# Transposed x in blocks of two tokens of one head, with the states doubled on the diagonal

## The chip, the core and the metric

The kernel runs on one core of a Trainium2 chip. TensorE (PE) multiplies matrices and transposes through an identity matrix; PEld is its weight load. VectorE (DVE) and ScalarE (ACT) do elementwise work and read results from PSUM, the matmuls' result memory. GpSimd (POOL) does elementwise work in SBUF and issues the DMA transfers that cast from float32 to bfloat16. SyncE (SP) issues the transposing transfers and nearly all stores of the output. Each engine works through its own queue in order and waits for the others by semaphores.

The metric is the device time of one execution in microseconds.

## The reference: what is computed

For batch b and head h (8 of each) x is 512 tokens by 64 and the state 32 rows by 64. Tokens read the state, state rows read the tokens; the two reads are joined, and a two-layer network with GELU follows.

```python
B, H, S, Ns, D = (8, 8, 512, 32, 64)
scores  = scale * x @ state^T ;  a  = softmax(scores)  ; xread = a  @ state
scores2 = scale * state @ x^T ;  a2 = softmax(scores2) ; sread = a2 @ x
rows = concat([xread, sread], tokens)          # 544 rows a batch, 8 heads x 64 = 512 columns
out  = gelu(rows @ w_in) @ w_out               # 512 -> 2048 -> 512
```

The exponential of the scores serves both reads. The token read is folded into the network: per batch P = state @ w_in (per head), and the hidden layer is the transposed attention times P.

## The kernel before

**Layout.** A batch of x is loaded by a casting transfer (`load_x`, POOL's queue) as `xb`: partition p holds tokens 4p to 4p+3 of all heads, so for each head 4 tokens times 64 columns lie in a row (`j` is the token within the four). Heads are numbered `4 t + c` with t in 0..1 and c in 0..3.

**Scores.** A score matmul wants the contraction over the 64 columns on the partitions; to use 128 partitions two heads are put together, t = 0 and t = 1 of the same c. `sbd` holds for each batch and c a block diagonal of 128 x 64: the transposed state of head c in rows 0 to 63 and columns 0 to 31, that of head 4 + c in rows 64 to 127 and columns 32 to 63. For the transposed x the pair has to lie side by side: `rearr` (L221) lets POOL copy `xb` into `x4` (two tiles in turn), two copies for a batch, and `xtr_dma` (L276) transposes `x4` in one transfer from SP's queue into `xT`. Batch 0 has a path of its own, batch 1 is transposed on TensorE by `xtr` (L264), in 32 transposes of 64 rows. Batches 2 to 7 go through `rearr` and `xtr_dma`. `scores` (L325) then does 16 matmuls of 64 columns for a batch into two PSUM tiles `pt`, and ACT takes the exponentials into `e`.

**States.** `load_st` loads states as `st_bf`; `state_prep` (L156) transposes a batch's states on TensorE in one transpose, and DVE copies the two halves out of PSUM (L166) into the two diagonal blocks of `sbd`. `p_mm` (L435) uses the blocks of `sbd` as weights against `w_in` for P. `sbd` is set to zero at the start by one POOL memset (L95).

**The rest of a batch.** DVE normalises the attention (`norm`), a second transposing transfer turns it (`atr_dma`), `M` computes two matmuls of the hidden layer for one of 16 slices and ACT's GELU, and `X` are the seven products of a Strassen form of the second layer, with the sums of the hidden layer on DVE (`g_sum`, L637), and a quarter in a second level (`sub_a`, `sub_b`, L727). `reads_mm` (L962) are the state reads, whose right operand `xo` is `xb` with columns of ones, copied by POOL (`rearr_ones`, L235). The state rows pass through the network at the end, with weight sums of `w_in` (`sr_w`), which before lie in `x4` for the names 1 and 6.

**Order.** It is written by hand: every engine gets its instructions in the program's order. Batches 0 and 1 run interleaved in a long prologue; from batch 2 on, a loop over eight stages (p = 0..7) for each batch b does two hidden slices per stage for b, products for b - 1, and scores, normalisation and P for b + 1. In the prologue `state_prep(2, 3)` stands between `U(13)` (output matmuls of batch 0, copied out by DVE at L519) and `M(20, 21)`; `state_prep(3, B)` prepares all the remaining batches behind `M(30, 31)`. Stage 4 of batch 2 has `M(40, 41)` alone; stage 5 has `M(42, 43)`, a product, the state reads (one PSUM tile `sr`, copied by ACT at L970), the P matmuls of batch 3 (copied at L1002 by ACT and DVE) and `sub_a`. Four PSUM tiles of `ps_f` go round in the order of allocation and hold the scores, the hidden slices, the transposed states, the state reads and part of P.

POOL's queue after its transfer issues is: the pair copies of batches 2 and 3, the ones copies of batch 3, a copy that waits for the transposed x of batch 2 (`hold`, L1181), the load of the states of batches 3 to 7 (L121), and then in each batch the next load of x, the pair copies and the ones copies, spaced by `hold` copies (L1016) that wait for a GELU.

Of the kernel before, what the change touches and what calls it, by code (L numbers as in the profile page):

```python
# [10 lines left out]
BF16 = mybir.dt.bfloat16  # L11
# [6 lines left out]
def kernel(  # L18
# [8 lines left out]
    nc = tc.nc  # L27
# [6 lines left out]
    HC = H // 2  # L34
# [34 lines left out]
    sbd = persist.tile([128, B, HC, 2 * NS], BF16, name="sbd")  # L69
# [6 lines left out]
    xT0 = persist.tile([128, 4, SJ, 128], BF16, name="xT0", tag="mix2")  # L76
    sb0 = persist.tile([128, 2, 2, 2, NS], BF16, name="sb0")
# [4 lines left out]
    x4s = [persist.tile([128, SJ, HC, 128], BF16, name=f"x4_{i}") for i in range(2)]  # L82
# [12 lines left out]
    nc.gpsimd.memset(sbd, 0.0)  # L95
# [38 lines left out]
    def load_rest():  # L134
        load_w_out(4, 6)
        load_w_out(6, 8)
        load_w_in(1024, 1536)
        load_w_out(8, 12)
        load_w_in(1536, 2048)
        load_st(2, 3)  # L140
        load_x(2)
        load_w_out(12, 16)
        load_x(3)

# [11 lines left out]
    def state_prep(b0, b1, pool=ps_f, tag="f"):  # L156
        n = b1 - b0
        ps = pool.tile([128, n, HC, NS], BF16, name="st_ps", tag=tag)
        for b in range(b0, b1):
            nc.tensor.transpose(  # L160
                ps[:, b - b0, :, :].rearrange("p c n -> p (c n)"),
                st_bf[:, b, :, :].rearrange("q t d -> q (t d)"),
                ident,
            )
        for t in range(2):
            nc.vector.tensor_copy(  # L166
                out=sbd[64 * t:64 * t + 64, b0:b1, :, 32 * t:32 * t + 32].rearrange(
                    "d b c n -> d (b c) n"
                ),
                in_=ps[64 * t:64 * t + 64, :, :, :].rearrange("d b c n -> d (b c) n"),  # L170
            )
# [23 lines left out]
    def state0_p(ps):  # L195
        for t in range(2):
            h = slice(64 * t, 64 * t + 64)
            nc.scalar.copy(out=sbd[h, 0, :, 32 * t:32 * t + 32], in_=ps[h, 2, :, :])
# [7 lines left out]
    def begin(b):  # L206
        A = Att()
        atts[b] = A
        A.x4 = x4s[b % 2]
        A.xo = xos[b % 2]  # L210
        if b > 0:
            A.xT = att.tile([128, SJ, HC, 128], BF16, name="xT", tag="xT")

# [6 lines left out]

    def rearr(b, ts=(0, 1)):  # L221
        A = atts[b]
        src = xbs[b].rearrange("p (t c) (j d) -> p t c j d", t=2, d=D)
        for t in ts:
            nc.gpsimd.tensor_copy(  # L225
                out=A.x4[:, :, :, 64 * t:64 * t + 64].rearrange("p j c d -> p c j d"),
                in_=src[:, t],
            )
# [35 lines left out]
    def xtr(b, cs):  # L264
        A = atts[b]
        xv = xbs[b].rearrange("p (t c) (j d) -> p j c t d", t=2, d=D)
        ps = ps_f.tile([128, len(cs), SJ, 128], BF16, name="xT_ps", tag="f")
        for i, c in enumerate(cs):
            for j in range(SJ):
                for t in range(2):  # L270
                    nc.tensor.transpose(ps[64 * t:64 * t + 64, i, j, :], xv[:, j, c, t, :], ident)
        nc.vector.tensor_copy(
            out=A.xT[:, :, cs[0]:cs[0] + len(cs), :].rearrange("p j c n -> p c j n"), in_=ps
        )

    def xtr_dma(b):  # L276
        A = atts[b]
        nc.sync.dma_start_transpose(
            out=A.xT.rearrange("p j c n -> p (j c) n"),
            in_=A.x4.rearrange("p j c n -> p (j c n)"),  # L280
        )
# [43 lines left out]
    def scores(b, half):  # L325
# [4 lines left out]
        for ci in range(2):  # L330
            c = 2 * half + ci
            for j in range(SJ):
                nc.tensor.matmul(  # L333
                    pt[:, j, :, ci, :],
                    lhsT=A.xT[:, j, c, :],
                    rhs=sbd[:, b, c, :],
                    start=True,
                    stop=True,
                )
# [95 lines left out]
    def p_mm(b, f, tiles):  # L435
# [3 lines left out]
        for c in range(HC):  # L439
            for t in range(2):  # L440
                nc.tensor.matmul(  # L441
                    ps[t][32 * c:32 * c + 32, :],
                    lhsT=sbd[64 * t:64 * t + 64, b, c, 32 * t:32 * t + 32],
# [36 lines left out]
    def pmat00(h):  # L480
# [3 lines left out]
        for c in range(HC):  # L484
            for t in range(2):
                nc.tensor.matmul(
                    ps[t][32 * c:32 * c + 32, :],
                    lhsT=sbd[64 * t:64 * t + 64, 0, c, 32 * t:32 * t + 32],
# [325 lines left out]
    def sr_w(name):  # L814
        if name in "52":
            homes = [opool.tile([128, 2, 512], BF16, name="srw", tag="osb") for _ in range(2)]
        elif name == "7":
            t = att.tile([128, 2, 2, 512], BF16, name="srw7", tag="xT")
            homes = [t[:, 0], t[:, 1]]
        else:  # L820
            t = x4s["16".index(name)].rearrange("p j c n -> p (j c n)")
            t = t.rearrange("p (g k f) -> p g k f", g=2, k=2)
            homes = [t[:, 0], t[:, 1]]
# [310 lines left out]
    state_prep(1, 2)  # L1134
# [6 lines left out]
    xtr(1, (0, 1))  # L1141
    xtr(1, (2, 3))
# [33 lines left out]
    rearr(2)  # L1176
    xtr_dma(2)
    begin(3)
    rearr(3)
# [7 lines left out]
    state_prep(2, 3, ps_o, "o3")  # L1187
# [26 lines left out]
    M(28, 29)  # L1214
    hold_for(1, 12)
    rearr_ones(2)
    M(30, 31)
    state_prep(3, B)
# [3 lines left out]
    for b in range(2, B):  # L1222
        nb = b + 1
        for p in range(8):
# [23 lines left out]
            if b == 2 and p == 1:  # L1248
                w_diff("7")
            if p < 5 and nb < B:  # L1250
# [24 lines left out]
            if p == 0 and nb + 1 < B:  # L1275
                begin(nb + 1)
                rearr(nb + 1)
# [42 lines left out]
    g_sum(b, "3", x4s[0].rearrange("p j (u c) n -> p (j u) (c n)", u=2))  # L1320
# [36 lines left out]
```

## Time and profile before

| | us |
|---|---|
| median of three runs | 202.26 (201.78 to 202.26) |
| profiled execution | 202.25 |
| its span in the profile | 200.3 |
| TensorE busy | 193.9 (97%) |
| VectorE busy | 155.1 (77%) |
| ScalarE busy | 145.6 (73%) |
| GpSimd busy | 48.1 (24%) |
| granted TensorE clock, mean | 1.00 |

Times in the trace are microseconds from the start of the span. Matmuls are pipelined, so an engine that shows as busy may still stand for part of the time; the chain of waits and the distance between matmuls say more. In a timeline row the columns are start, duration, engine, line and operation, output and inputs with their shapes, the number of instructions merged into the row, and in brackets how long the engine stood before it and what ended that. In a row of groups there are busy time and mean duration after the bar.

### The profile page before, as it was taken

Reading aid. Unit: us, or ns where it says so; the run is one execution under the profiler, and the core shown is the slowest. Engines: PE = TensorE matmul, PEld = TensorE weight load, DVE = VectorE, ACT = ScalarE, POOL = GpSimd, SP = SyncE. Lnnn points to the kernel's source line nnn. Section 1 sums busy time; section 2 is a strip of 40 time slices with the busy share of each in tenths; the row PEclk is TensorE's granted clock in tenths of the full one; section 3 lists DMA queues with packets and bytes.
Section 4 is the critical chain, followed back from the end, with each engine's and each line's share of the span. In section 5 each row is a group of like instructions: output and inputs, shape, how many; then the busy total and the mean of one; then the engine's idle time right before and its main releaser. Section 6 shows DMA issues by size and latency. Waiting matters only on the chain.

```text
span 200.3 us, 5055 instructions
## 1 busy us (share of the span) xinstructions
PE 193.9 (97%) x2102; PEld 134.3 (67%) x2107; DVE 155.1 (77%) x279; ACT 145.6 (73%) x264; POOL 48.1 (24%) x65
## 2 busy tenths in 40 slices
PE   7899999999999999999999999999999999999993
PEld 2533544465767777767777787677776888878893
DVE  2963796969989769975997798849966897984863
ACT  3785577699896799569966997599948778775120
POOL 8972504543403444040504300030000000000000
PEclk9999999999999999999999999999999999999999
DMA  5999999976494959680797025420024010030044
GB/s 192 197 174 202 206 199 201 183 136 142 84 149 77 241 65 164 141 214 0 77 188 209 5 67 95 138 75 27 28 107 106 0 55 0 7 153 0 18 146 157
DMA packets 40567, 23.16 MB, mean 116 GB/s; under 512 B 21856, under 2 KB 39136, under 8 KB 40544
## 3 DMA queue, kind: packets, MB, share of 16 engines
q0 software_dynamic: 13984, 8.10, 29.9%
q1 hardware_dynamic: 25728, 14.22, 27.5%
q10 hardware_dynamic: 832, 0.52, 0.8%
q8 instruction: 16, 0.26, 0.5%
q14 instruction: 7, 0.06, 0.1%
HBM read 17.30 MB, written 8.91 MB: 131 GB/s over the span
## 4 chain that ended last, share of the span: by engine, by line
PE 86%; DMA 5%; POOL 4%; ACT 2%; issue 0%; DVE 0%; POOLq 0%
PE xp L647 36%; PE hp L506 26%; DMA xb<-in_x_dram 5%; PE xp L727 5%; PE op L548 3%; PE sp L866 3%; PE rp L932 3%; POOL w_in_bf L105 2%; PE op L532 2%; PE xp L773 2%; PE pt L333 2%; ACT P L1002 1%; PE p_ps L441 1%; PE sr L962 1%; POOL sbd L95 1%; POOL w_out_bf L113 1%
## 5 line engine op out<-in xcount | busy, mean ns | idle before, releaser
L513 ACT ACTIVATE g<-hp 128x512 bf16<-128x512 f32 x124 | 67.1, 614 | 17.0 <-PE hp L506 16.8
L506 PE MATMUL hp<-AT,P 128*128 128x512 bf16 x248 | 62.2, 379 | 0.0
L647 PEld LDWEIGHTS <-gsum 128*128 128x128 bf16 x416 | 40.4, 98 | 8.9 <-issue 0.4
L647 PE MATMUL xp<-ws,gsum 128*128 128x256 bf16 x320 | 38.2, 273 | 0.0
L506 PEld LDWEIGHTS <-P 128*128 128x128 bf16 x248 | 23.0, 98 | 19.4 <-ACT P L452 0.7
L647 PEld LDWEIGHTS <-g 128*128 128x128 bf16 x240 | 23.3, 98 | 4.8
L637 DVE TENSOR_TENSOR gsum<-g 128x2048 bf16<-128x2048 bf16 x14 | 17.0, 1218 | 0.6 <-ACT g L513 0.6
L225 POOL COPY x<-xb 128x1024 bf16<-128x1024 bf16 x12 | 12.2, 1044 | 18.5 <-DMA xb<-in_x_dram 18.5
L235 POOL COPY xo<-xb 128x1024 bf16<-128x1024 bf16 x12 | 12.2, 1043 | 14.1 <-PE sr L962 13.9
L647 PE MATMUL xp<-w_out_bf,g 128*128 128x256 bf16 x128 | 15.3, 273 | 0.0
L647 PE MATMUL xp<-ws,g 128*128 128x256 bf16 x112 | 13.4, 273 | 0.0
L1016 POOL COPY hold<-g 128x1 bf16<-128x1 bf16 x7 | 2.3, 334 | 42.9 <-ACT g L513 42.9
L666 DVE TENSOR_TENSOR c<-qb 128x256 f32<-128x256 f32 x6 | 2.6, 425 | 12.7 <-ACT qb L749 12.7
L548 PE MATMUL op<-w_out_bf,g 128*128 128x512 bf16 x44 | 11.0, 380 | 0.5 <-issue 0.3
L647 PE MATMUL xp<-w_out_bf,gsum 128*128 128x256 bf16 x96 | 11.5, 273 | 0.0
L666 DVE TENSOR_TENSOR oh<-xp,c 128x512 f32<-128x512 f32 x14 | 9.6, 686 | 2.4 <-PE xp L647 2.0
L1002 DVE CAST P<-p_ps 128x512 bf16<-128x512 f32 x15 | 9.4, 683 | 2.4 <-PE p_ps L441 2.4
L356 DVE TENSOR_TENSOR a<-e,ics 128x512 bf16<-128x512 bf16 x14 | 10.5, 750 | 0.5
L353 DVE TENSOR_REDUCE cs<-e 128x16 f32<-128x512 bf16 x14 | 9.5, 678 | 0.9 <-ACT e L340 0.9
L513 ACT ACT_TABLE_LOAD x7 | 9.0, 1283 | 0.1
L441 PE MATMUL p_ps<-w_in_bf,sbd 64*32 64x512 bf16 x248 | 9.0, 380 | 0.0
L637 DVE TENSOR_TENSOR gsum<-gsum,g 128x2048 bf16<-128x2048 bf16 x7 | 8.6, 1225 | 0.2
(155 smaller groups left out, 308.9 us busy)
## 6 DMA issues: line engine op xcount, KB each, us to landing
out_dram<-oh SPq DMA_DIRECT2D x15, 256.0 KB, 3.3
xb<-in_x_dram POOLq DMA_DIRECT2D x7, 512.0 KB, 7.1
out_dram<-oh SPq DMA_DIRECT2D x6, 512.0 KB, 3.1
w_in_bf<-in_moe_w_in_dram POOLq DMA_DIRECT2D x6, 256.0 KB, 11.7
out_dram<-osb SPq DMA_DIRECT2D x5, 256.0 KB, 3.0
w_out_bf<-in_moe_w_out_dram POOLq DMA_DIRECT2D x4, 256.0 KB, 7.8
w_out_bf<-in_moe_w_out_dram POOLq DMA_DIRECT2D x2, 512.0 KB, 13.3
x0f<-in_x_dram SPq DMA_DIRECT2D x3, 256.0 KB, 3.8
```

Of the source, the lines that this page charges most:

```text
L225: nc.gpsimd.tensor_copy(out=A.x4[:, :, :, 64 * t:64 * t + 64].rearrange("p j c d -> p c j d"), in_=src[:, t],)
L235: eng.tensor_copy(out=A.xo[:, :, :, 2 + 64 * t:66 + 64 * t].rearrange("p j c d -> p c j d"), in_=src[:, t],)
L356: nc.vector.tensor_tensor(out=A.a[:, :, hs].rearrange("p g (c n) -> p g c n", n=NS), in0=e4, in1=ics[:, :, :].to_broadcast((128, G, 2, NS) ...
L441: nc.tensor.matmul(ps[t][32 * c:32 * c + 32, :], lhsT=sbd[64 * t:64 * t + 64, b, c, 32 * t:32 * t + 32], rhs=w_in_bf[64 * t:64 * t + 64, c ...
L506: nc.tensor.matmul(hp, lhsT=Ps[b][:, t, m * 128:(m + 1) * 128], rhs=atts[b].AT[:, :, t, :], start=(t == 0), stop=(t == 1),)
L513: nc.scalar.activation(out=gs[b][:, m, :], in_=hp, func=AF.Gelu)
L548: nc.tensor.matmul(ops[b, j], lhsT=gs[b][:, m, j * 128:(j + 1) * 128], rhs=w_out_bf[:, m, :], start=(m == 0), stop=(m == MC - 1),)
L637: nc.vector.tensor_tensor(out=got[name], in0=x, in1=y, op=op)
L647: nc.tensor.matmul(ps[:, j - js[0], :], lhsT=lhs[:, m, 128 * j:128 * j + 128], rhs=rhs[:, m, :], start=(first and j == js[0] and m == 0), ...
L666: nc.vector.tensor_tensor(out=out, in0=x, in1=y, op=ALU.add)
L727: nc.tensor.matmul(xs[b, 0][:, at, :], lhsT=lhs[:, m, :], rhs=rhs[:, m, :], start=(start and m == 0), stop=(m == MH // 2 - 1), skip_group_ ...
L1002: copy(out=Ps[b][:, t, f * 512:(f + 1) * 512], in_=ps[t])
```

## The change

The transposing transfer reads `xb` itself. A block of 128 columns of `xb` holds two tokens of one head (64 columns each), so its transpose has token 2q of the head in rows 0 to 63 and token 2q + 1 in rows 64 to 127. For both halves to meet the state of that head, the state lies twice on the diagonal: `sbd` now has a block diagonal for each of the eight heads instead of four pairs, twice the size. The number and shape of the score matmuls stay; a score matmul now yields two tokens of one head. `rearr` and `x4` are gone.

To get a state into both halves, `state_twice` copies `st_bf` into `st2` with every state doubled: on DVE for batch 1 and for batch 2, right ahead of their transposes in the program, and on POOL for batches 3 to 7. `state_prep` then does two transposes for a batch instead of one. The preparation of batches 3 to 7 is split: batch 3 where all five were, batches 4 to 7 in stage 4 of batch 2, behind `M(40, 41)`, and there the second half is copied by ACT. The second half of `sbd` is set to zero by POOL behind `load_x(3)`. The batch-1 transposes on TensorE are 16 of 128 rows. The weight sums that lay in `x4` go to `st_bf` and an attention buffer (name 6) and to a new tile `late4` (name 1), which the last sum of the hidden layer uses too.

```diff
-    sbd = persist.tile([128, B, HC, 2 * NS], BF16, name="sbd")
+    sbd = persist.tile([128, B, H, 2 * NS], BF16, name="sbd")
+    st2 = persist.tile([128, B - 3, 2, 2, D], BF16, name="st2")
-    x4s = [persist.tile([128, SJ, HC, 128], BF16, name=f"x4_{i}") for i in range(2)]
+    late4 = persist.tile([128, 4, 512], BF16, name="late4")
-    nc.gpsimd.memset(sbd, 0.0)
+    nc.gpsimd.memset(sbd[:, 0:B // 2], 0.0)
...
         load_x(3)
+        nc.gpsimd.memset(sbd[:, B // 2:B], 0.0)
...
+    def state_twice(b0, b1, eng):
+        eng.tensor_copy(
+            out=st2[:, 0:b1 - b0].rearrange("q b t u d -> q (b t) u d"),
+            in_=st_bf[:, b0:b1].rearrange("q b t d -> q (b t) d")[:, :, None, :].broadcast_to(
+                [128, 2 * (b1 - b0), 2, D]
+            ),
+        )
-    def state_prep(b0, b1, pool=ps_f, tag="f"):
+    def state_prep(b0, b1, base, pool=ps_f, tag="f"):
         n = b1 - b0
-        ps = pool.tile([128, n, HC, NS], BF16, name="st_ps", tag=tag)
+        ps = pool.tile([128, n, H, NS], BF16, name="st_ps", tag=tag)
...
+        for b in range(n):
+            for t in range(2):
+                nc.tensor.transpose(
+                    ps[:, b, HC * t:HC * t + HC, :].rearrange("p c n -> p (c n)"),
+                    st2[:, b0 - base + b, t].rearrange("q u d -> q (u d)"),
+                    ident,
+                )
+        for u in range(2):
+            copy = nc.scalar.copy if n > 1 and u else nc.vector.tensor_copy
+            copy(
+                out=sbd[64 * u:64 * u + 64, b0:b1, :, 32 * u:32 * u + 32].rearrange(
+                    "d b h n -> d (b h) n"
                 ),
+                in_=ps[64 * u:64 * u + 64, :, :, :].rearrange("d b h n -> d (b h) n"),
             )
...
-    def rearr(b, ts=(0, 1)):
...
-    def xtr(b, cs):
+    def xtr(b, hs):
...
+        for i, h in enumerate(hs):
+            for q in range(SJ // 2):
+                nc.tensor.transpose(ps[:, i, q, :], xbs[b][:, h, 128 * q:128 * q + 128], ident)
+        nc.vector.tensor_copy(out=A.xT[:, hs[0]:hs[0] + len(hs)], in_=ps)
     def xtr_dma(b):
         nc.sync.dma_start_transpose(
-            out=A.xT.rearrange("p j c n -> p (j c) n"),
-            in_=A.x4.rearrange("p j c n -> p (j c n)"),
+            out=A.xT.rearrange("p h q n -> p (h q) n"),
+            in_=xbs[b].rearrange("p h d -> p (h d)"),
         )
...
-            c = 2 * half + ci
-            for j in range(SJ):
+            for t in range(2):
+                h = HC * t + 2 * half + ci
+                for q in range(SJ // 2):
                 nc.tensor.matmul(
-                    pt[:, j, :, ci, :],
-                    lhsT=A.xT[:, j, c, :],
-                    rhs=sbd[:, b, c, :],
+                        pt[:, 2 * q:2 * q + 2, t, ci, :],
+                        lhsT=A.xT[:, h, q, :],
+                        rhs=sbd[:, b, h, :],
...
+        elif name == "6":
+            homes = [
+                st_bf.rearrange("q (k b) t d -> q k (b t d)", k=2),
+                att.tile([128, 2, 512], BF16, name="srw6", tag="a"),
+            ]
...
-            t = x4s["16".index(name)].rearrange("p j c n -> p (j c n)")
+            homes = [late4[:, 0:2], late4[:, 2:4]]
...
-    state_prep(1, 2)
+    state_twice(1, 2, nc.vector)
+    state_prep(1, 2, 1)
...
-    rearr(2)
     xtr_dma(2)
     begin(3)
-    rearr(3)
     rearr_ones(3)
...
     U(13)
-    state_prep(2, 3, ps_o, "o3")
+    state_twice(2, 3, nc.vector)
+    state_prep(2, 3, 2, ps_o, "o3")
     M(20, 21)
...
     M(28, 29)
+    state_twice(3, B, nc.gpsimd)
     hold_for(1, 12)
     rearr_ones(2)
     M(30, 31)
-    state_prep(3, B)
+    state_prep(3, 4, 3)
...
+            if b == 2 and p == 4:
+                state_prep(4, B, 3)
...
-                rearr(nb + 1)
```

## The prediction

> **What bounds the kernel now.** I read the page's busy shares, then the chain that ended last, then single engines in time around the places that the change touches.
>
> Page, parts 1 and 4:
>
> ```profile
> PE 193.9 (97%) x2102; PEld 134.3 (67%) x2107; DVE 155.1 (77%) x279; ACT 145.6 (73%) x264; POOL 48.1 (24%) x65
> ...
> PE 86%; DMA 5%; POOL 4%; ACT 2%; issue 0%; DVE 0%; POOLq 0%
> ```
>
> TensorE is 86% of the chain; the 4% POOL and 5% DMA are one stretch at the start (memset, weight issues, the load of x[1], which lands at 19.4 us). Behind that the chain is TensorE to the end. So POOL's work is beside the path, and what counts is any moment when TensorE's in-order queue stands.
>
> The first such moment is batch 2's state preparation. TensorE, then DVE (start, us, engine, line):
>
> ```profile
> 37.60 1.04 PE L532 MATMUL op<-w_out_bf,g 128*128 128x512 bf16 x4
> 38.47 0.22 PE L160 MATMUL st_ps<-ident,st_bf 128*128 128x128 bf16 x1
> 38.53 1.89 PE L506 MATMUL hp<-AT,P 128*128 128x512 bf16 x8
> ```
>
> ```profile
> 34.62 1.23 DVE L576 TENSOR_TENSOR ws<-w_out_bf 128x2048 bf16<-128x2048 bf16 x1 [0.24 <-DMA w_out_bf<-in_moe_w_out_dram]
> 35.88 1.22 DVE L576 TENSOR_TENSOR ws<-w_out_bf,ws 128x2048 bf16<-128x2048 bf16 x1
> 37.15 0.69 DVE L519 COPY osb<-op 128x512 f32<-128x512 f32 x1
> 37.76 1.28 DVE L453 CAST P<-p_ps 128x512 bf16<-128x512 f32 x2
> 38.95 0.68 DVE L519 COPY osb<-op 128x512 f32<-128x512 f32 x1
> 39.55 0.45 DVE L166 COPY sbd<-st_ps 64x128 bf16<-64x128 bf16 x2
> ```
>
> TensorE goes from output matmuls through the state's transpose to the next without a pause, because the transpose reads loaded data. DVE is without a pause from 34.62 to 40.0 and runs about 1 us behind TensorE; its row of work begins when the last part of w_out lands (0.24 us of waiting).
>
> The second is stage 5 of batch 2 (DVE, then ACT):
>
> ```profile
> 60.10 1.29 DVE L453 CAST P<-p_ps 128x512 bf16<-128x512 f32 x2 [0.71 <-PE p_ps L441]
> 61.30 1.83 DVE L637 TENSOR_TENSOR gsum<-g,gsum 128x2048 bf16<-128x2048 bf16 x1
> 63.05 0.68 DVE L666 TENSOR_TENSOR oh<-xp,s 128x512 f32<-128x512 f32 x1
> 63.65 0.68 DVE L666 TENSOR_TENSOR oh<-xp,c 128x512 f32<-128x512 f32 x1
> ...
> 65.71 0.68 DVE L666 TENSOR_TENSOR oh<-xp,u 128x512 f32<-128x512 f32 x1
> ```
>
> ```profile
> 62.54 2.06 ACT L513 ACTIVATE g<-hp 128x512 bf16<-128x512 f32 x4 [1.28 <-PE hp L506]
> 66.40 0.38 ACT L970 COPY sraw<-sr 128x260 f32<-128x260 f32 x1 [1.80 <-PE sr L962]
> 66.75 1.56 ACT L1002 CAST P<-p_ps 128x512 bf16<-128x512 f32 x3
> ```
>
> DVE has a backlog there until 66.4; ACT is ahead and waits for TensorE (1.28 and 1.80 us). TensorE's matmuls run without a gap across this stretch.
>
> **The change part by part.**
>
> *Copies of x go.* Twelve POOL copies:
>
> ```profile
> L225 POOL COPY x<-xb 128x1024 bf16<-128x1024 bf16 x12 | 12.2, 1044 | 18.5 <-DMA xb<-in_x_dram 18.5
> ```
>
> 12 x 1.04 us leave POOL, which is 24% busy and off the path: 0. Cover isn't needed. The transposing transfers on SP can start 2.0 us earlier (x[2]: 34.19 to about 32.2); their readers are placed by TensorE's order (scores of batch 2 at 41.77, with no wait), so no gain. Nothing stands behind the transfer on SP before 37.87. DVE gains a little: its two-input operations were stretched when a POOL copy ran (1826 against 1218 ns at 61.30, 1509 against 692 at 78.04, 1962 against 682 near batch 4's weight sums): 0.61 + 0.82 + 1.28 = 2.7 us of DVE, which is 0% of the chain: 0. The Trainium skill ("SBUF — State Buffer", Who interferes with whom) says that a DVE instruction with two SBUF inputs is locked out while a GpSimd instruction reads SBUF; these rows agree with it, and by that rule alone, were DVE the pace, the kernel would gain 2.7 us.
>
> *TensorE work.* State transposes go from 7 to 14; five took 0.44 us and one 0.22, so 55 ns for each further one. By place: +1 at 14.8, +1 at 38.5, -3 at 48.3 (two instead of five), +8 at 62.8: +0.39 us. x[1]: 32 half-width transposes took 1.08 us, 28 ns each; 16 full ones at the 56 ns of the attention transposes (8 in 0.61 us) take 1.06: 0. Scores and P keep number and shape.
>
> *Batch 1's states (14.8 us).* The new doubling copy on DVE falls into its 1.77 us of idleness. The two copies out of PSUM are 64x256: 64x128 takes 220 ns and 64x640 takes 483, so 286, +0.13 in all before the next weight load. TensorE then waited 0.23 us for x[1] to land, which hides it: +0.05 (0 to 0.2).
>
> *Batch 2's states (38.5 us).* The doubling copy is a DVE instruction, and in the built program it stands behind both output copies and the P casts; TensorE's transposes wait for it, and all matmuls behind them in its queue too. DVE comes to it at 39.55. Price of 128x256: the nearest rows are a 128x512 bf16 copy at 350 ns and a 64x128 one at 220; I take 0.25. From DVE's end to TensorE's start 0.05 to 0.22 us (other handovers: 6.03 to 6.08, 15.85 to 16.07). So 39.55 + 0.25 + 0.2 = 40.0 instead of 38.47, and one transpose more: +1.6 (1.4 to 1.75). ACT (which waits for these matmuls, 0.57 us) and DVE move along, so nothing is won back. The clock shows 1.00 here. "TensorE: Matmul & The Clock Gate" (What's actually happening) lets the clock fall after an idle window of about 3.4 us; 1.6 us is short of it; were it to fall, some 3.4 us at half speed would add 1.7.
>
> *The earlier transfer.* The DMA engines are saturated until 36 us. In the trace's packet records the transposed x[2] moves from 35.7 to 39, and while x[3] ran beside it, x[3]'s packets fell from 366 to 278 in a microsecond. Two microseconds earlier it meets the last 1.0 us of w_out, whose landing starts DVE's row of work above. Ends: 0, and 2.2 us (the whole transfer's time when alone, 37 to 39). I take 0.4, near the tail's own length: of that 1 us, less than half is lost to sharing. DVE, and through it the wait above, shift by this.
>
> *States 3 to 7.* The POOL doubling copy (1280 elements at 1.04 us per 1024: 1.3) follows their load, issued at 41.40, landed by 46; with the pair copies gone it can be issued at about 39.5. TensorE asks at 48.1: hidden, by 2 us even if x[3] lands 1 us later. Three transposes fewer here: -0.17. The second half of the memset (1.80 us on POOL) lies in its 7.31 us of waiting before 32.15: 0.
>
> *States 4 to 7, now in stage 4 of batch 2.* Eight transposes between matmul pairs (+0.44), into one of the four rotating PSUM buffers; then a DVE copy of one half and an ACT copy of the other, and ACT's waits for DVE's (the built program's semaphore says so). ACT's next two GELUs, then the read-out copy and the P copies stand behind it. In times of before: DVE's sum takes 1.22 with POOL's copy gone, so DVE reaches the copy at 65.1; 64x1024 at 0.51 ns per element, 0.68: 65.8. ACT's half: 128x256 takes 372 ns and 128x512 some 590, so 1.0: 66.9. Two GELUs (0.51 each): 67.95; the read-out copy: 68.3; the first P copy: 68.85. The P matmuls need these buffers in this order, and the quarter products, at 67.39 before, need the first P copy: 69.0. +1.6, the 0.44 included (0.44 if DVE's copy comes at once; 2.2 if the sum stays at 1.83).
>
> *New homes for weight sums* (state buffer, an attention buffer, a new tile): the attention buffer's last reader is a transfer issued at 127.58, landing within 4.8; the sum is at 138.8: 0.
>
> Sum: 0.05 + 1.6 + 0.4 - 0.17 + 1.6 = +3.5. The profiled execution took 202.25 us (span 200.3), the median is 202.26, so 205.7.
>
> **The rivals.**
> - *One of the two waits is covered*: 204.2 without batch 2's wait (0.05 + 0.06 + 0.4 - 0.17 + 1.6 = 1.9), 204.6 if ACT's late GELUs cost only the transposes (2.3). For it: ACT had 3.1 us of idle time in that stage. Against: the buffers rotate in order, so TensorE meets that delay at the next P.
> - *Nothing waits*: only TensorE's count stays, +0.39: 202.6, within the bound. It needs DVE to reach the doubling copy by 38.2, 1.3 us earlier than its row of work allows.
> - *Faster*: DVE, relieved of POOL's copies, sets the pace somewhere that the chain doesn't show; 2.7 us of stretched operations less 0.39: 199.9. It decides if the stretched operations gate TensorE; against it, TensorE has no gap behind any of them.
> - *The transfer delays w_out's tail by up to its whole 2.2 us*: 205.7 + 1.8 = 207.5. For it: saturated engines; against: only the tail is left by then.
>
> **How the numbers follow.** Forecast 0.62; one wait covered 0.15; long collision 0.13; nothing waits 0.05; faster 0.05. A difference under 0.3% (0.6 us) can't be told from no change. Slower: 0.62 + 0.15 + 0.13 = 0.90; same 0.05; faster 0.05. All low ends together give +1.7 (203.9), all high ends +6.2 (208.4); with the covered wait below and the long collision above I take 203.6 to 207.8.
>
> **What would show it.** TensorE idle of 1.4 us or more before the transposes of batch 2's states, ended by DVE; ACT idle some 2 us in stage 4 of batch 2, ended by DVE's copy into sbd, then P matmuls waiting for ACT; x[2]'s transposing transfer issued near 32 us; DVE's three stretched operations back at 1218, 692 and 682 ns; from stage 6 of batch 2 on, the same spacing as before, shifted. The forecast is wrong if TensorE shows no wait at either place, or if its stages 3 to 7 get shorter.

## The result, and the profile after

The changed kernel takes 205.39 us (204.91 to 205.83) beside 202.06 us for the kernel before on the same chip: 1.0165 times as long, with a 95% interval of 1.0136 to 1.0195. It is slower, by 3.3 us. The forecast was 205.7. The profiled execution took 205.57 us with a span of 203.6, against 202.25 and 200.3.

Page of the changed kernel, parts 1 and 4:

```profile
PE 195.5 (96%) x2093; PEld 135.0 (66%) x2098; DVE 153.8 (76%) x282; ACT 146.6 (72%) x265; POOL 39.3 (19%) x55
...
PE 83%; DVE 8%; ACT 4%; DMA 2%; issue 1%
```

POOL lost 8.8 us of work and DVE 1.3, which moved nothing. TensorE is busy for 1.6 us longer, but its share of the chain fell from 86% to 83%, and DVE, 0% before, now has 8% and ACT 4% instead of 2%: other engines hold TensorE up. The timelines show where. TensorE of the changed kernel, at three places (start, us, engine, line and operation, the bracket is the time for which it stood):

```profile
37.20 1.04 PE L531 MATMUL op<-w_out_bf,g 128*128 128x512 bf16 x4
39.42 0.28 PE L171 MATMUL st_ps<-ident,st 128*128 128x128 bf16 x2 [1.19 <-DVE st L159]
...
49.33 0.28 PE L171 MATMUL st_ps<-ident,st 128*128 128x128 bf16 x2
50.44 1.91 PE L646 MATMUL xp<-ws,g 128*128 128x256 bf16 x16 [0.84 <-DVE P L1215]
...
63.84 1.03 PE L505 MATMUL hp<-AT,P 128*128 128x512 bf16 x4
64.70 0.61 PE L171 MATMUL st_ps<-ident,st 128*128 128x128 bf16 x8
...
69.42 1.33 PE L440 MATMUL p_ps<-w_in_bf,sbd 64*32 64x512 bf16 x24 [0.21 <-ACT g L512]
70.68 0.62 PE L726 MATMUL xp<-w_out_bf,g 128*128 128x128 bf16 x8
```

The same places in the kernel before, as far as the prediction did not show them:

```profile
48.31 0.44 PE L160 MATMUL st_ps<-ident,st_bf 128*128 128x128 bf16 x5
48.59 0.60 PE L647 MATMUL xp<-ws,g 128*128 128x256 bf16 x4
...
61.91 1.89 PE L506 MATMUL hp<-AT,P 128*128 128x512 bf16 x8
67.39 0.61 PE L727 MATMUL xp<-w_out_bf,g 128*128 128x128 bf16 x8
```

From starts like these the whole difference can be added up. Each distance is a start less an earlier start.

| stretch of TensorE's queue | before | after | difference |
|---|---|---|---|
| start to the output matmuls `U(13)` | 37.60 | 37.20 | -0.40 |
| `U(13)` to the transposes of batch 2's states | 0.87 | 2.22 | +1.35 |
| to the transposes of batch 3's states | 9.84 | 9.91 | +0.07 |
| to the products `X(1, "4")` of batch 1 | 0.28 | 1.11 | +0.83 |
| to `M(40)`, stage 4 of batch 2 | 13.32 | 13.40 | +0.08 |
| `M(40)` to the quarter products `sub_a`, stage 5 | 5.48 | 6.84 | +1.36 |
| to the end of the span | 132.9 | 132.9 | 0 |

The sum is +3.29, which is the difference of the spans. Three stretches carry it. The first and the third are waits that the prediction has; the middle one, 0.83 us, it does not have.

DVE of the changed kernel at these places:

```profile
33.67 1.36 DVE L575 TENSOR_TENSOR ws<-w_out_bf 128x2048 bf16<-128x2048 bf16 x1
...
38.55 0.68 DVE L518 COPY osb<-op 128x512 f32<-128x512 f32 x1
39.15 0.22 DVE L159 COPY st<-st_bf 128x256 bf16<-128x256 bf16 x1
39.74 0.59 DVE L178 COPY sbd<-st_ps 64x256 bf16<-64x256 bf16 x2 [0.38 <-PE st_ps L171]
...
45.28 1.77 DVE L355 TENSOR_TENSOR a<-e,ics 128x512 bf16<-128x512 bf16 x1
...
63.24 1.22 DVE L636 TENSOR_TENSOR gsum<-g,gsum 128x2048 bf16<-128x2048 bf16 x1
...
67.03 0.68 DVE L178 COPY sbd<-st_ps 64x1024 bf16<-64x1024 bf16 x1
```

The doubling copy (39.15) runs only 0.22 us, but stands at the end of DVE's row of work, and TensorE starts 0.05 us behind it. The multiplication at 45.28 takes 1.77 us; the same line takes 0.69 where nothing disturbs it. What disturbs it is POOL's doubling copy of batches 3 to 7, as two experiments below show by taking it out. On POOL's timeline:

```profile
45.25 1.25 POOL L159 COPY st<-st_bf 128x1280 bf16<-128x1280 bf16 x1 [5.26 <-DVE ics L354]
```

It started 0.03 us earlier. The P casts behind that multiplication in DVE's queue come 1.1 us late, and the products of batch 1 wait for them (0.84 in the bracket above). ACT in stages 4 and 5 of batch 2:

```profile
64.47 1.08 ACT L512 ACTIVATE g<-hp 128x512 bf16<-128x512 f32 x2 [1.28 <-PE hp L505]
67.74 1.01 ACT L178 COPY sbd<-st_ps 64x1024 bf16<-64x1024 bf16 x1 [2.18 <-DVE sbd L178]
68.77 1.08 ACT L512 ACTIVATE g<-hp 128x512 bf16<-128x512 f32 x2
69.74 0.38 ACT L972 COPY sraw<-sr 128x260 f32<-128x260 f32 x1
70.00 1.60 ACT L1004 CAST P<-p_ps 128x512 bf16<-128x512 f32 x3
```

ACT stands 2.18 us for DVE's copy, and two GELUs, the copy of the state reads and the P copies follow in a row without a pause, the quarter products behind them.

### The profile page after: what moved, and what is told of

It is laid out like the page before. It is cut to its first block, busy times and chain, and to the rows that moved or that the text cites. A ratio compares the mean times of both kernels' runs of the same rounds, so it can differ in the third digit from the quotient of the medians.

```text
span 203.6 us, 5041 instructions
## 1 busy us (share of the span) xinstructions
PE 195.5 (96%) x2093; PEld 135.0 (66%) x2098; DVE 153.8 (76%) x282; ACT 146.6 (72%) x265; POOL 39.3 (19%) x55
## 4 chain that ended last, share of the span: by engine, by line
PE 83%; DVE 8%; ACT 4%; DMA 2%; issue 1%
PE xp L646 33%; PE hp L505 24%; PE op L547 5%; PE xp L726 5%; PE sp L868 3%; PE rp L934 3%; PE xp L772 2%; DMA st_f<-in_state_dram 2%; PE pt L332 1%; PE p_ps L440 1%; DVE P L452 1%; DVE a L355 1%; ACT g L512 1%; ACT P L1004 1%; PE xT_ps L259 1%
## 5 line engine op out<-in xcount | busy, mean ns | idle before, releaser
L440 PE MATMUL p_ps<-w_in_bf,sbd 64*32 64x512 bf16 x248 | 9.9, 380 | 0.3 <-ACT g L512 0.2
L451 ACT CAST P<-p_ps 128x512 bf16<-128x512 f32 x9 | 4.9, 590 | 4.8 <-PE p_ps L440 4.8
```

The source lines that it names most:

```text
L440: nc.tensor.matmul(ps[t][32 * c:32 * c + 32, :], lhsT=sbd[64 * t:64 * t + 64, b, HC * t + c, 32 * t:32 * t + 32], rhs=w_in_bf[64 * t:64 * ...
```

## The experiments

Three theories stood at first. A: TensorE's in-order queue sets the pace, and the change put separate waits into it, each of which can be taken out by itself. B: DVE's row of work is the pace, and the waits overlap, so that taking one out lets another show. C: the new layout itself is dearer, by its scores, transposes or transfers. Later two more were about the transfer (D and N, below). Times beside a run are of the same chip as the kernel before that the ratio refers to.

**The doubling copy of batch 2 early.** It is put ahead of the row of work, where DVE has time; nothing else changes.

```diff
     M(12, 13)
+    state_twice(2, 3, nc.vector)
     srt(1)
...
     U(13)
-    state_twice(2, 3, nc.vector)
     state_prep(2, 3, 2, ps_o, "o3")
```

> Only edit against the changed kernel: the DVE copy that doubles batch 2's states stands ahead of the transpose of batch 1's state read, where DVE stood idle for 1.6 us, instead of behind the two output copies. Theory A (TensorE's queue sets the pace, and the change put three separate waits into it: 1.35 us for this copy, 0.83 us for P casts that a POOL copy made late, 1.36 us in stage 4 and 5 of batch 2): the wait ahead of the state transposes near 39.4 us goes, the other two stay, time 1.35 us below the changed kernel's 205.4, so 204.0. Theory B (DVE's row of work is the pace and the waits overlap): TensorE starts these transposes earlier and waits as much longer further on; 205.0 to 205.4. Theory C (the new layout itself is dearer): 205.4.

Measured: 203.62 us (203.29 to 204.1), ratio 1.0067 (1.0041 to 1.0093). TensorE:

```profile
37.16 1.04 PE L531 MATMUL op<-w_out_bf,g 128*128 128x512 bf16 x4
38.03 0.28 PE L171 MATMUL st_ps<-ident,st 128*128 128x128 bf16 x2
```

The distance is 0.87 us as before the change, with no bracket. The stretch of stages 4 and 5 stays 6.84, so nothing came back there: this is A, and B falls. The span of this profile is 201.5, 2.1 less than with the change alone: 1.35 is this wait, and 0.77 more lies in the distance to the products of batch 1, 0.34 instead of 1.11, of which the edit says nothing; the last table of this section comes back to it.

**Both halves of the states of batches 4 to 7 copied by DVE.** ACT's copy goes; the eight transposes stay in stage 4.

```diff
-            copy = nc.scalar.copy if n > 1 and u else nc.vector.tensor_copy
+            copy = nc.vector.tensor_copy
```

> Only edit against the changed kernel: in stage 4 of batch 2 DVE copies both halves of the states of batches 4 to 7 out of PSUM, ACT none. Theory A: ACT's two GELUs no longer stand behind DVE's copy, the PSUM buffer comes free about 0.65 us after DVE's first copy, about when the P matmuls ask for it, and the quarter products start about 0.9 us earlier than in the changed kernel; the eight transposes (0.44 us) stay. 204.5. If it is the transposed states' hold on one of four rotating PSUM buffers and not ACT's wait: under 0.3 us, 205.2. Theory B: 205.0 to 205.4. Theory C: 205.4.

Measured: 204.76 us (204.16 to 204.94), ratio 1.0108 (1.0049 to 1.0167). TensorE, then ACT:

```profile
63.95 1.03 PE L505 MATMUL hp<-AT,P 128*128 128x512 bf16 x4
...
69.79 0.61 PE L726 MATMUL xp<-w_out_bf,g 128*128 128x128 bf16 x8
```

```profile
65.89 1.08 ACT L512 ACTIVATE g<-hp 128x512 bf16<-128x512 f32 x2 [0.23 <-PE hp L505]
```

The stretch falls from 6.84 to 5.84. ACT reaches its second pair of GELUs without standing for DVE. What is left over the 5.48 of before is 0.36, less than the 0.44 us of the eight transposes. The rival that the transposed states are dear by their hold on one of the four PSUM tiles (expected: under 0.3) falls with it: the tile comes free 4.57 us behind `M(40)` instead of 4.91, only 0.34 earlier. In this profile DVE stood 1.15 us for w_out and its doubling copy took 0.32, so that the first wait was 0.88 longer (3.10 us from `U(13)` to the transposes), and the distance to the products of batch 1 was 0.81 shorter; these nearly cancel, and the span of 202.7 is 0.9 below that of the changed kernel, about the 1.00 of the stretch.

**States of batches 3 to 7 loaded twice.** Two casting loads put them straight into `st2`, which grows by a batch, and POOL's doubling copy goes.

```diff
-    load_st(3, B)
+    load_st_twice(3, B, 1)
...
-    state_twice(3, B, nc.gpsimd)
...
-    state_prep(3, 4, 3)
+    state_prep(3, 4, 2)
```

```diff
+    def load_st_twice(b0, b1, at):
+        for u in range(2):
+            nc.gpsimd.dma_start(
+                out=st2[:, at:at + b1 - b0, :, u, :].rearrange("q b t d -> q (b t) d"),
+                in_=st_rows[:, b0:b1, :, :].rearrange("q b t d -> q (b t) d"),
+            )
```

> Only edit against the changed kernel: the states of batches 3 to 7 are loaded twice, straight into the doubled tile, so POOL's copy of 1280 elements is gone; one load more (about 1 us of POOL's issue time). Theory A, that POOL's copy at 45.25 us shut out a DVE operation with two SBUF inputs (1.77 us instead of 0.69) and so made P casts late: that operation is back at 0.69 us, TensorE's wait of 0.84 us near 50.4 us goes, 204.5. If the casts are late for another reason: the operation is short, the wait stays, 205.4. If the second load lands later than 49 us, the transposes of batch 3's states wait for it instead.

Measured: 204.96 us (204.53 to 205.66), ratio 1.0129 (1.0076 to 1.0181). The distance to the products of batch 1 is 0.11 us, 0.17 below the kernel before: the three transposes fewer that the prediction counted. The multiplication is back at its usual time:

```profile
46.40 0.69 DVE L362 TENSOR_TENSOR a<-e,ics 128x512 bf16<-128x512 bf16 x1
```

The time fell by only 0.4, which the two intervals can't tell from nothing, and the profiled run, 205.66, is the slowest of its four. DVE and TensorE show where the gain went:

```profile
35.30 1.23 DVE L582 TENSOR_TENSOR ws<-w_out_bf 128x2048 bf16<-128x2048 bf16 x1 [0.97 <-DMA w_out_bf<-in_moe_w_out_dram]
```

```profile
37.55 1.04 PE L538 MATMUL op<-w_out_bf,g 128*128 128x512 bf16 x4
40.54 0.28 PE L178 MATMUL st_ps<-ident,st 128*128 128x128 bf16 x2 [1.95 <-DVE st L166]
```

DVE stood 0.97 us for w_out before its row of work, and the wait at batch 2's states took over what was won: 2.99 from `U(13)` instead of 2.22 (and `U(13)` itself began 0.35 later, by the loads). Of these 0.77 us, DVE's later arrival is 0.60 and the doubling copy itself 0.16: it took 0.38 us for 0.22, beside POOL's ones copies, and ended 0.08 us behind them. So the first wait has no fixed length; it goes with w_out's landing and with where POOL's ones copies fall.

**All three together.** The early copy, the double load, and the preparation of batches 4 to 7 in stage 6 of batch 2 by DVE alone.

```diff
-            if b == 2 and p == 4:
-                state_prep(4, B, 3)
...
             if p == 6:
+                if b == 2:
+                    state_prep(4, B, 2)
                 sub_b(b)
```

> The edits of the early doubling copy and of the double load together, and the preparation of batches 4 to 7 moved to stage 6 of batch 2, both halves on DVE, which stood idle there for 1.8 us. Theory A: all three waits go, of the whole change TensorE's seven more transposes (0.39 us) are left: 202.5, within the bound of the kernel before. Theory B: another wait of 0.5 us or more shows up and the time stays above 203.3. Theory C: 204 or more with no wait of TensorE to show for it.

Measured: 202.14 us (201.9 to 203.29), ratio 0.9993 (0.9966 to 1.002): the kernel before, within what can be told. The layout, with its 16 score matmuls, its doubled states and its direct transposing transfers, then costs at most 0.2% (0.4 us) by this interval, so C does not explain the 3.3 us. It wins nothing that can be told either. TensorE:

```profile
37.25 1.04 PE L538 MATMUL op<-w_out_bf,g 128*128 128x512 bf16 x4
38.13 0.27 PE L178 MATMUL st_ps<-ident,st 128*128 128x128 bf16 x2
...
48.02 0.28 PE L178 MATMUL st_ps<-ident,st 128*128 128x128 bf16 x2
48.13 1.91 PE L653 MATMUL xp<-ws,g 128*128 128x256 bf16 x16
...
61.51 1.89 PE L512 MATMUL hp<-AT,P 128*128 128x512 bf16 x8
66.90 0.61 PE L733 MATMUL xp<-w_out_bf,g 128*128 128x128 bf16 x8
```

The spacings are 0.88, 0.11 and 5.39, and the eight transposes cost 0.45 in stage 6.

**The transfer late again.** Two questions were open: whether the transposing transfer of x[2], issued earlier, delays w_out (D) or not (N), and how far the distances repeat. Here POOL copies x[2] first, as before the change.

```diff
-    xtr_dma(2)
+    for i in range(2):
+        nc.gpsimd.tensor_copy(out=pair[:, 1024 * i:1024 * i + 1024], in_=flat[:, 1024 * i:1024 * i + 1024])
+    nc.sync.dma_start_transpose(
+        out=atts[2].xT.rearrange("p h q n -> p (h q) n"), in_=pair
+    )
```

(`pair` is `late4` and `flat` is `xbs[2]`, both as two-dimensional views.)

> The changed kernel, but two POOL copies put x[2] into a tile first and the transposing transfer of batch 2 reads that tile, so that it is issued about 2 us later, as before the change; the other batches are as changed. Theory D (the earlier transfer takes time from the tail of w_out, which starts DVE's row of work): the wait of VectorE's weight sums for w_out shrinks, the time falls by 0.4 to 0.9 us below the changed kernel, 204.5 to 205.0. Theory N (the transfer's packets start only after the last of w_out whenever it is issued, and w_out's landing varies by the loads themselves): no difference to the changed kernel beyond 0.3 us, 205.1 to 205.7, and the packets of the transfer start after the last ones of w_out in both.

The changed kernel beside it:

> The changed kernel once more, for a second profile. If the waits are made by the program's order, the spacing of stages 4 and 5 of batch 2 is 6.84 us again and the wait before the transposes of batch 2's states is between 1.3 and 2.2 us, longer by as much as w_out lands later. If the late second-layer products of batch 1 (0.83 us, the multiplication of VectorE beside GpSimd's doubling copy) hang on which of the two starts first, that spacing may be anything from 0.2 to 0.9 us here. Time 205.4 within 0.4.

Measured: 206.13 us (204.87 to 206.65) with the late transfer, 206.16 (205.57 to 207.43) without; 1.0187 (1.0155 to 1.0219) and 1.0206 (1.0173 to 1.0239). There is no difference, which speaks for N; with four runs each, spread over nearly 2 us, an effect of 0.4 could hide. DVE waited for w_out with the late transfer too (the second row is SyncE's issue of the transfer):

```profile
35.93 1.23 DVE L575 TENSOR_TENSOR ws<-w_out_bf 128x2048 bf16<-128x2048 bf16 x1 [0.60 <-DMA w_out_bf<-in_moe_w_out_dram]
35.51 3.04 SPq L1183 DMA_TRANSPOSE xT<-late  x1
```

Over the profiles of this study DVE's wait for w_out was 0.24, 0.27 and 0.60 us with the late transfer, and between 0 and 1.15 with the early one (0 four times, 0.24, 0.40, 0.51, 0.93, 0.97, 1.10, 1.15). The traces' packet records say whether the two meet. With the late transfer w_out's last packet ends at 35.64 us and the transfer's first starts at 36.79; in the changed kernel the two are at 33.34 and 34.29. In its second profile they lie side by side for 0.9 us, from 35.67 on, with 159 of the transfer's 2048 packets. In the nine other profiles with the early transfer at most 12 of the 2048 start before w_out's end, and none does in the one where DVE stood longest for w_out (1.15 us, both halves by DVE). So w_out lands late by itself, which speaks against D; but "only after the last of w_out whenever it is issued", as N had it, is not so in every execution, and a price for the overlap is not shown.

The time of the changed kernel, 206.16, is above the 205.4 within 0.4 that was expected; the kernel before was spread on that chip too, from 201.81 to 205.18. The second profile of the changed kernel (`after_again`) has the first and third stretch again, 2.26 and 6.84, and the middle one is gone. TensorE:

```profile
39.99 1.04 PE L531 MATMUL op<-w_out_bf,g 128*128 128x512 bf16 x4
42.25 0.28 PE L171 MATMUL st_ps<-ident,st 128*128 128x128 bf16 x2 [1.22 <-DVE st L159]
...
52.15 0.27 PE L171 MATMUL st_ps<-ident,st 128*128 128x128 bf16 x2
52.26 1.91 PE L646 MATMUL xp<-ws,g 128*128 128x256 bf16 x16
```

The distance is 0.11: there the POOL copy began at 48.56, 0.46 us after a multiplication had begun, which then took its usual 0.69. Its span was longer all the same, 205.5, because everything in the prologue came late: x[1]'s transposes began at 21.8 us instead of 19.03, the last part of x[0] having landed late (DVE stood 1.45 us for it at 8.48).

**The kernel before, a second profile.** 202.04 us (201.75 to 202.3).

> The kernel before once more, for a second profile: x[1]'s transposes start at 19.41 us in its first profile and at 19.0 in most of the changed ones. If that is variation of the loads, it starts between 19.0 and 19.4 here; if it comes from GpSimd's memset at the start, which is half as long after the change, it is 19.4 again. Time 202.2 within 0.4.

x[1]'s transposes begin at 19.23, between the 19.41 of its first profile and the 19.03 of the changed kernel: variation of the loads. `U(13)` begins at 37.43 there and at 37.53 in the third profile of the changed kernel, so the -0.40 of the first row of the table is no gain of the change. The memset at the start runs 1.80 us in both, half of a tile twice as large.

**Three waits mended, less memset.** POOL zeroes only batch 0 of `sbd` at the start, DVE batch 1, POOL the rest later, so that w_in's loads are issued 1.28 us earlier.

```diff
-    nc.gpsimd.memset(sbd[:, 0:B // 2], 0.0)
+    nc.gpsimd.memset(sbd[:, 0:1], 0.0)
+    nc.vector.memset(sbd[:, 1:2], 0.0)
...
-        nc.gpsimd.memset(sbd[:, B // 2:B], 0.0)
+        nc.gpsimd.memset(sbd[:, 2:B], 0.0)
```

> The kernel with the three waits mended, and GpSimd zeroes only the first batch's diagonal at the start, VectorE the second, GpSimd the rest behind the issue of x[3]. If the memset at the head of the chain gates the landing of x[1], its transposes start 0.5 to 0.8 us earlier than in the kernel with three waits mended and the time is 201.3 to 201.8; if the loads themselves do, it stays at 202.1 within 0.3.

Measured: 203.42 us (201.55 to 204.8), ratio 1.0038 (1.0008 to 1.0068). Neither expectation holds: the runs are spread over 3 us (the kernel before, on the same chip, over 3.4), and x[1]'s transposes began later in the profile, at 20.6. DVE, at the start:

```profile
8.42 0.43 DVE L253 CAST x0b<-x0f 128x512 bf16<-128x512 f32 x1 [1.71 <-DMA x0f<-in_x_dram]
```

The last part of x[0] landed late, as in the second profile of the changed kernel, where the memset was untouched. Whether issuing w_in earlier makes that happen more often is left open. No version beat the kernel before.

**The place alone.** Preparation of batches 4 to 7 in stage 6, ACT's copy kept.

```diff
-            if b == 2 and p == 4:
-                state_prep(4, B, 3)
...
             if p == 6:
+                if b == 2:
+                    state_prep(4, B, 3)
                 sub_b(b)
```

> The changed kernel with one edit: the preparation of the states of batches 4 to 7 stands in stage 6 of batch 2, ahead of the second half of the quarter products, and ScalarE still copies the second half. In the profile with three waits mended VectorE is free in that stage, and its first copy starts 0.2 us behind the transposes. If the place behind VectorE's backlog is what costs (theory A), stages 4 and 5 take 5.4 to 5.5 us from the hidden slices to the quarter products instead of 6.84, stage 6 gains the transposes' 0.44, and the time is 0.7 to 1.0 us below the changed kernel in the same call. If ScalarE's copy ahead of its GELUs costs the same in any stage, the time is that of the changed kernel within 0.4 us.

Beside it the changed kernel a third time:

> The changed kernel a third time, beside the two others on the same chip. The wait before the transposes of batch 2's states is 2.2 to 2.5 us from the start of the output matmuls, stages 4 and 5 of batch 2 take 6.84 us; time 205.4 to 206.2.

Measured: 204.86 us (203.82 to 204.89) against 205.3 (204.98 to 206.0); ratios 1.0125 (1.0095 to 1.0155) and 1.0164 (1.0136 to 1.0192). TensorE, ACT and DVE of the kernel with the moved preparation:

```profile
63.91 1.89 PE L505 MATMUL hp<-AT,P 128*128 128x512 bf16 x8
...
69.31 0.61 PE L726 MATMUL xp<-w_out_bf,g 128*128 128x128 bf16 x8
...
71.06 0.61 PE L171 MATMUL st_ps<-ident,st 128*128 128x128 bf16 x8
```

```profile
72.98 1.01 ACT L178 COPY sbd<-st_ps 64x1024 bf16<-64x1024 bf16 x1
```

```profile
71.78 0.68 DVE L178 COPY sbd<-st_ps 64x1024 bf16<-64x1024 bf16 x1 [0.22 <-PE st_ps L171]
74.63 0.43 DVE L665 TENSOR_TENSOR c<-qb 128x256 f32<-128x256 f32 x1 [2.17 <-ACT qb L748]
```

The stretch is 5.40, 1.44 less, and stage 6 takes 0.45 more: about 1.0 won in the trace. The same copy by ACT stands there without a wait, because DVE's copy starts 0.22 us behind the transposes; DVE then waits 2.17 us for ACT, and TensorE does not notice. So it is the place behind DVE's backlog that cost, as A has it. The gain of 0.44 between the medians is below the expected 0.7 to 1.0. The profiles say what stood against it: beside the third one of the changed kernel, x[1]'s transposes began 0.49 later and the first wait was 0.30 longer, while the distance to the products of batch 1 was 0.56 shorter; with the 1.0 of the edit that makes 0.8, as the spans of 202.8 and 203.6 have it.

**Two waits mended, POOL's copy kept.** The early copy, and stage 6 by DVE alone.

```diff
     M(12, 13)
+    state_twice(2, 3, nc.vector)
     srt(1)
...
-    state_twice(2, 3, nc.vector)
     state_prep(2, 3, 2, ps_o, "o3")
...
-            copy = nc.scalar.copy if n > 1 and u else nc.vector.tensor_copy
+            copy = nc.vector.tensor_copy
...
-            if b == 2 and p == 4:
-                state_prep(4, B, 3)
...
             if p == 6:
+                if b == 2:
+                    state_prep(4, B, 3)
                 sub_b(b)
```

> The changed kernel with the doubling copy of batch 2 early and the states of batches 4 to 7 prepared in stage 6 by VectorE alone; GpSimd's doubling copy of batches 3 to 7 stays. By theory A the two largest waits go: 202.3 us, and 0.1 to 0.8 more where GpSimd's copy happens to start together with VectorE's multiplication. If the waits overlap (theory B), one of them stays hidden behind the other and the time is above 203.3.

Measured: 202.47 us (202.02 to 203.4), ratio 1.0034 (1.0016 to 1.0052). Both waits are gone but for 0.16 us (1.03 for 0.87, and 5.39 for 5.48), which is A's number and not B's. Its ten runs lie at 202.0 to 202.5 and at 203.1 to 203.4. A second profile of the same kernel was to say why:

> The kernel with two waits mended once more, for a second profile. Its runs lay at 202.0 to 202.5 and at 203.1 to 203.4 us, and the profiled one (202.02) had 0.17 us from the transposes of batch 3's states to the products of batch 1. If GpSimd's doubling copy beside VectorE's multiplication makes the difference, a run above 203.0 shows 0.7 us or more there, and a run at 202.0 to 202.5 shows at most 0.4. If x[1]'s landing makes it, its transposes start about 1 us later in a run above 203.0 and the distance is as short in both.

It took 202.32 us with a distance of 0.12 to the products of batch 1, so an upper one was not caught, and what makes them is not settled.

**The POOL copy beside DVE's multiplication**, read across these profiles. End of POOL's copy is its start plus its duration; the multiplication is the one of the same line that meets it.

| profile | POOL's copy ends | multiplication starts, takes | it ends after POOL's copy by | to the products of batch 1 |
|---|---|---|---|---|
| after | 46.50 | 45.28, 1.77 | 0.55 | 1.11 |
| after, third | 46.42 | 45.64, 1.32 | 0.54 | 0.67 |
| early doubling copy | 45.97 | 45.49, 1.02 | 0.54 | 0.34 |
| both halves by DVE | 46.63 | 46.21, 0.95 | 0.53 | 0.30 |
| two mended | 45.78 | 45.45, 0.87 | 0.54 | 0.17 |
| late transfer | 47.15 | 46.87, 0.82 | 0.54 | 0.17 |
| two mended, second | 45.97 | 45.78, 0.74 | 0.55 | 0.12 |
| after, second | 49.91 | 49.71, 0.74 | 0.54 | 0.11 |
| place alone | 45.99 | 46.41, 0.69 | no overlap | 0.11 |

The multiplication ends 0.53 to 0.55 us after POOL's copy whenever it starts, so all but some 0.15 us of its 0.69 comes behind POOL's end. The kernel before shows the same: the multiplication at 78.04 (1.51 us) ends 0.55 us behind a pair copy of POOL, and the sum at 61.30, which takes 1.22 alone, 1.08 behind another. Some 0.1 us of the delay is absorbed before TensorE waits. Without the POOL copy (three mended, double load) it takes 0.69 and the distance is 0.11. In the profile "two mended, second" an earlier multiplication began 0.09 us ahead of POOL's copy, and there the copy took 1.71 us for 1.25:

```profile
44.17 0.69 DVE L355 TENSOR_TENSOR a<-e,ics 128x512 bf16<-128x512 bf16 x1
44.26 1.71 POOL L159 COPY st<-st_bf 128x1280 bf16<-128x1280 bf16 x1 [3.51 <-DVE ics L354]
```

## Why the prediction was right, and where it was not

The time was right: 205.39 for 205.7, well inside the range, and later runs of the changed kernel at 206.16 and 205.3. Its two main waits are there, with the engines that it named. One term of the sum had the wrong sign, and one was not shown.

- **What bounds the kernel.** Right. TensorE's queue adds up to the span, each wait could be taken out by itself, and 8.8 us less on POOL bought nothing. DVE's stretched sum at 61.30 took 1.22 after (63.24), as said, the two others are back at 0.69 and 0.68 us, and no stage became shorter for it: the faster rival falls.
- **Batch 2's states, +1.6.** Right in mechanism, and 1.35 plus 0.06 for the further transpose in the profile; 1.39 and 1.38 in the other two profiles of the changed kernel for the distance. DVE came to the copy 1.95 us after `U(13)`, exactly the distance taken from the profile before (39.55 less 37.60). The 0.2 us of handover to TensorE was the mis-sized part: it was 0.05, the low end of the rows named. ACT and DVE had nothing to win back. What sets these 1.95 us is not w_out, as the prediction had it, but TensorE itself: in the changed kernel DVE's first output copy (36.75) stood 0.46 us for `U(12)`, the output matmuls ahead of `U(13)`.
- **The earlier transfer, +0.4.** Not shown. The transfer was issued at 31.12, early as forecast, but DVE's row of work began at 33.67 without a wait for w_out, earlier than the 34.62 of before, and the late transfer gave the same time as the early one. The reading under it does not hold either: with the late transfer x[3]'s packets fell alike, from 182 to 96 per half microsecond between 35.0 and 36.5 us, before the transfer's first (36.79), so x[3] runs out by itself. And DVE does not shift with w_out one for one: with 0 or 0.24 us of waiting for it DVE still comes to the copy 1.95 us behind `U(13)`, and only with 0.60, 0.97 and 1.15 us (late transfer, double load, both halves by DVE) at 2.19, 2.55 and 2.73. The term stood for something real of another cause: w_out's landing moves by itself, POOL's ones copies stretch the doubling copy, and by both the first wait goes from 2.22 to 3.10 us between `U(13)` and the transposes.
- **States 3 to 7, -0.17.** Wrong, this is the step that failed. The prediction called POOL's doubling copy hidden, because TensorE asks for its result only at 48.1; its result was early indeed. But a copy also acts on what runs beside it: it shut out DVE's multiplication, and the distance became +0.83 longer instead of 0.17 shorter (+0.39 in the third profile, -0.17 in the second). The prediction had quoted the rule for the copies that go, and did not apply it to the one that comes. The Trainium skill ("SBUF — State Buffer", Who interferes with whom) says that a DVE instruction with two SBUF inputs contends with a GpSimd instruction that reads SBUF, and that the order of issue decides which of them is blocked. The table above agrees: where POOL's copy began first, the multiplication ended 0.53 to 0.55 us behind it, in eight profiles; where a multiplication began 0.09 us ahead, POOL's copy took 1.71 us for 1.25.
- **States 4 to 7, +1.6.** Right: +1.36, in three profiles 6.84, 6.84 and 6.85. By the prediction's steps, in times of before (1.93 less): DVE's copy at 65.10 for 65.1, ACT's copy done at 66.82 for 66.9, both GELUs done at 67.92 for 67.95. The 0.25 too much came at the end, where the copy of the state reads and the first P copy were added as durations although the second starts 0.26 us after the first; the quarter products came at 68.75 for 69.0. The copies' prices, 0.68 and 1.01 for 0.68 and 1.0, held.
- **Costed at nothing.** The 16 full transposes of x[1] take 1.06 as said, the second memset runs at 24.42 inside POOL's waiting, and the new homes of the weight sums cost nothing: from the quarter products of batch 2 to the end the distances are equal to 0.1. The 0.05 at batch 1's states is below what the loads vary by.

So the sum of 3.5 met 3.3 because errors cancelled: 0.2 and 0.25 too much in the waits, 0.4 for a transfer's collision that was not seen and 0.4 of luck in the loads, against 1.0 too little at POOL's copy. In the third profile the same span of 203.6 came from other parts: -0.07 from the loads and +0.39 at the products of batch 1.

## What to carry to other kernels

An engine whose queue is in order charges a short new instruction by its place, not by its length: a 0.22 us copy cost 1.4 us at the end of another engine's row of work and nothing a few instructions earlier. Before calling work on an idle engine hidden, look not only for who needs its result, but also for what runs beside it: a GpSimd copy of 1.25 us shut out a two-input instruction of VectorE, and its price swung between 0 and 1 us with some tenths of a microsecond of timing. Where two engines copy halves of one tile and one waits for the other, put the pair where the engine that copies first has no backlog.

## What the runs showed of the hardware

- A multiplication of VectorE with two inputs in SBUF (0.69 us alone) does not slow down in proportion beside a GpSimd copy that began first: it ends 0.53 to 0.55 us behind that copy, whether they overlapped for 0.2 or 1.2 us (eight profiles); the other way round, a GpSimd copy that started 0.09 us behind such a multiplication took 1.71 us instead of 1.25. VectorE's plain doubling copy waited too: in four profiles it took 0.25, 0.32, 0.38 and 0.54 us instead of 0.22 beside POOL's ones copies and ended 0.08 us behind them.
- A transposing transfer that is issued earlier did not land earlier while casting loads filled the DMA engines. The one of x[2] held SyncE's queue for 4.8 to 5.2 us when issued early and for 3.04 to 3.16 behind POOL's copies, and by the packet records its last packet ended 19.4 to 19.7 us behind the start of x[1]'s transposes when issued late (three profiles) and 19.0 to 20.4 when issued early (ten of eleven profiles; 18.1 in the kernel with less memset).
- The loads of the prologue vary from execution to execution: x[1]'s transposes began between 18.8 and 21.8 us, which moves the whole time.
- TensorE's granted clock stayed at 1.00 through waits of up to 2.1 us.
